# Expert blocks in a straight line, further blocks listed on the chip

## The chip, the cores and the metric
The kernel runs on one core of a Trainium2 chip. TensorE (PE) multiplies, VectorE (DVE), ScalarE (ACT) and GpSimd (POOL) work on elements, SyncE (SP) issues most transfers. The metric is the device time of one execution in microseconds; the median of three runs of the kernel before is 744.07 us (741.57 to 744.4).

## The reference
Causal attention (2 batches, 12 heads, 448 positions, 64 wide), then a dense layer pair with a sigmoid gate, then a routed layer with eight experts, one for each token. The last part is what the change touches:

```
logits = x @ w_gate;  e_idx = argmax(logits, axis=1)        # 896 tokens, 8 experts
gate_w = softmax(logits)[e_idx];  eom = sigmoid(x @ w_output_gate)
for e in range(8):
    mask = e_idx == e
    h = maximum(x[mask] @ w1[e], 0)      # 768 -> 1024
    out[mask] = gate_w[mask] * eom[mask, e] * (h @ w2[e])   # 1024 -> 768
```

With the inputs of the runs the experts get 189, 5, 2, 48, 222, 30, 58 and 342 tokens.

## The kernel before
Attention and the dense layers run to about 404 us and stay as they are. Their output `y1_d` lies in DRAM; beside it DRAM holds a list `xl_d` with 896 places for each expert, into which `place` scatters token number and weight of each 128 tokens as they are routed.

An expert's work comes in **blocks** of up to 128 tokens (`block`, L805). A block gathers its token rows by a list (`gather`, into `xw` or `xr`), transposes them and splits them into a high and a low float32r part (`prep`, into `xh`, `xl`). The weights of an expert are twelve units `u` of 512 KB: six of `w1`, six of `w2` (four of 512 columns, two of 256). A unit is loaded by SP into one of 24 places, so two experts are on the chip (`load32`), and split into a high and a low part in one of six pairs of buffers, `ent` and `entb` (`split`, L275): a cast to float32r, for five units on POOL (L279) and for seven on ACT (L281), and a subtraction on DVE (L282). `l1` multiplies xh by high, xh by low and xl by high (L834, L838); `relu` goes to `hs`, `tr` transposes it and splits it into `hh` and `hl` (L851), and `l2m` does the second product (L858, L860). The output is scaled and scattered to `out` by POOL (L892).

The first block takes the first tokens of expert 0 among the first 640 tokens, before routing is complete (`lw0`), and the other tokens of expert 0 come after it (`le0`). For each expert `rest(o, i)` is an If: where an expert has more than 128 tokens left, a further block runs inside it, with another nested If behind it for the next 128. The count of further blocks of all experts is packed into one number, read into a register of every engine (`load_counts`), and each branch has a prefetch hint some units ahead (`hint`). Then the expert's last block runs, which reloads each place with the weights of the expert after next. Further blocks thus run while their expert's weights are on the chip, and load nothing.

Each engine runs its instructions in the order written, and waits for others by semaphores; POOL's casts, gathers and scatters share one line, and so do DVE's subtractions for weights, for `hl` and for the small operations of routing. Splits run three units ahead of a block, two more at its start.

Of the kernel before, what the change touches and what calls it, by code (L numbers as in the profile page):

```python
# [107 lines left out]
def kernel(ctx, tc, q, k, v, w_in, w_out, w_gate, w_og, w1, w2, out):  # L108
    nc = tc.nc
# [23 lines left out]
    SPLIT_AT = (0, 6, 13)  # L133
    BIG = 65536
    CUT = 5
    POOL_HI, AHEAD, OVER = (3, 5, 7, 9, 11), 5, 3
# [22 lines left out]
    with tc.manual_schedule():  # L159
# [92 lines left out]
        def src_of(e, u):  # L252
            if u < 6:
                hf, kk = u // 3, u % 3 * 2
                return w1[e, kk * 128:(kk + 2) * 128, hf * 512:(hf + 1) * 512].rearrange("(a p) n -> p a n", p=128), 2
            g4, r = (u - 6) // 3 * 4, (u - 6) % 3
            if r < 2:
                kk = g4 + 2 * r
                return w2[e, kk * 128:(kk + 2) * 128, 0:512].rearrange("(a p) n -> p a n", p=128), 2
            return w2[e, g4 * 128:(g4 + 4) * 128, 512:768].rearrange("(a p) n -> p a n", p=128), 4  # L260
# [3 lines left out]

        def load32(o, u):
# [9 lines left out]
        def split(o, u):  # L275
            raw = places[(NU * o + u) % NR]
            hi, lo = entries[u % NENT]
# [213 lines left out]
        for fq in range(4):  # L491
            for fc in range(4):
# [13 lines left out]
                if f == 15:  # L506
                    es_x.close()
                    mp = ctx.enter_context(pool("moe2"))
                    xw_t = [mp.tile([128, DM], F32, name="xw0")]
                    lw_t = [mp.tile([128, NE, 2], I32, name=f"lwin{i}") for i in range(2)]  # L510
                    lr_t = [mp.tile([128, 2], I32, name=f"lr{i}") for i in range(2)]
                    lgB = mp.tile([64, TT, 128], F32, name="lgB")
                    es_gg, ggp = opened(pool("gsplit"))
# [159 lines left out]
        def xpair(n):  # L673
            pl = wp if n else mp
            return [pl.tile([128, KD, 128], F32R, name=f"x{c}{n}") for c in "hl"]

        def prep(xw, pair):
            xh, xl = pair
            for hf in range(2):
                p = ps.tile([128, 4, 128], F32, name="ps_x", tag="tp", bufs=2)  # L680
                for c in range(3):
                    kk = 3 * hf + c
                    nc.tensor.transpose(p[:, c], xw[:, kk * 128:(kk + 1) * 128], ident)
                dst = xh[:, 3 * hf:3 * hf + 3]
                nc.scalar.copy(dst, p[:, 0:3])
                nc.vector.tensor_sub(xl[:, 3 * hf:3 * hf + 3], p[:, 0:3], dst.bitcast(F32))
# [3 lines left out]
        xm = xpair(0)  # L690
# [6 lines left out]
        ix = [mp.tile([128, 1], I32, name=f"ix{i}") for i in range(2)]  # L697

        def cut_count():
# [5 lines left out]
            nc.vector.tensor_scalar(pos0, pos0, c0_f, float(NT * e0), op0=ALU.add, op1=ALU.add)  # L705

        def rest_list(i, lw):
            x = ix[i % 2]
            nc.vector.tensor_scalar(x, pos0, float(128 * i), None, op0=ALU.add)
            nc.vector.memset(lw, BIG)  # L710
            nc.gpsimd.indirect_dma_start(
                out=lw, out_offset=None, in_=xl_d[:, :],
                in_offset=bass.IndirectOffsetOnAxis(ap=x.bitcast(U32), axis=0),
                bounds_check=NT * (e0 + 1) - 1, oob_is_err=False)
# [10 lines left out]
        for t in range(TT):  # L725
# [25 lines left out]
            def h15(t=t):  # L751
                if t == TT - 1:
                    prep(xw_t[0], xm)

            hooks = dict(zip(R_AT, (h2, h5, h7, h10, h15)))
            if t == TT - 1:
                for u, kk in enumerate(SPLIT_AT):
                    hooks[kk] = lambda u=u: split(0, u)
# [5 lines left out]
        xr = wp.tile([128, DM], F32, name="xr")  # L764
        nc.gpsimd.memset(xr, 0.0)
        xx = xpair(1)
# [10 lines left out]
        def rest_lists():  # L777
            rest_list(0, le0)
            rest_list(1, lr_t[1])
            for i in range(2):  # L780
                nc.gpsimd.dma_start(lw_t[i], xl_d.rearrange(
                    "(e r) c -> r e c", e=NE)[128 * i:128 * (i + 1)])


        ci = mp.tile([128, 1], I32, name="ci")

        def counts():
            p = ps.tile([128, 2 * NE], F32, name="ps_tot", tag="sm", bufs=2)
            nc.tensor.matmul(p[:, 0:NE], ones, acc[TT], start=True, stop=True)
            cf = mp.tile([128, NE], F32, name="cf")  # L790
            cw = mp.tile([128, NE], F32, name="cw")
            xf = mp.tile([128, 1], F32, name="xf")
            nb = mp.tile([128, NE], I32, name="nb")
            nc.vector.tensor_add(cf, p[:, 0:NE], cbase)
            nc.vector.tensor_sub(cf[:, e0:e0 + 1], cf[:, e0:e0 + 1], c0_f)
            nc.vector.tensor_copy(nb, cf)
            nc.vector.tensor_scalar(nb, nb, 7, None, op0=ALU.logical_shift_right)
            nc.vector.tensor_copy(cw, nb)
            nc.vector.tensor_mul(cw, cw, pw8)
            nc.vector.tensor_reduce(xf, cw, axis=AX.X, op=ALU.add)  # L800
            nc.vector.tensor_copy(ci, xf)
# [3 lines left out]
        def block(o, pair, lw, final, hooks):  # L805

            xh, xl = pair
            hs = hs_t[npass[0] % 2]
# [7 lines left out]
            def step(u):  # L816
                v = u + AHEAD
                if v < NU:
                    split(o, v)
                    if final and o + 2 < NE:  # L820
                        load32(o + 2, v)
                elif v - NU >= OVER:
                    return
                elif not final:
                    split(o, v - NU)
                elif o + 1 < NE:
                    split(o + 1, v - NU)

            def l1(u):
                hf, k0 = u // 3, u % 3 * 2  # L830
                hi, lo = entries[u % NENT]
                for n in range(2):
                    for m, wt in enumerate((hi, lo)):
                        nc.tensor.matmul(hps[hf], xh[:, k0 + n], wt[:, n], start=k0 + n == 0 and m == 0, stop=False)  # L834
                    if n == 0:
                        hook((hf, k0))
                for n in range(2):
                    nc.tensor.matmul(hps[hf], xl[:, k0 + n], hi[:, n], start=False, stop=k0 + n == KD - 1)  # L838
# [14 lines left out]
            def l2m(py, u, n, kks):  # L853
                hi, lo = (t.rearrange("p a n -> p (a n)").rearrange("p (b n) -> p b n", n=n)
                          for t in entries[u % NENT])
# [6 lines left out]
            for v in range(AHEAD):  # L862
                if v >= OVER:
                    split(o, v)
                if final and o + 2 < NE:
                    load32(o + 2, v)
# [30 lines left out]

        def windows(o):
            return (nblk >> (3 * ORDER[o])) & 7

        def hint(o, i):
            tc.mark_branch_hint_location(f"more{o}_{i}", hint=(windows(o) + (7 - i)) >> 3, engines=engs)

        def rest(o, i):
            with tc.If(windows(o) > i, label=f"more{o}_{i}"):  # L905
                e = ORDER[o]
                lw = lr_t[i % 2] if o == 0 or i > 1 else lw_t[1][:, e]
                prep(xr, xx)
                hooks = {}
                if i + 1 < TT:  # L910
                    lnx = lr_t[(i + 1) % 2]

                    def h0():
                        if o == 0:
                            rest_list(i + 1, lnx)
                        else:
                            window(e, i + 1, lnx)

                    hooks[0, 3] = h0
                    hooks[1, 3] = lambda: gather(lnx, xr)  # L920
                    hooks[6] = lambda: hint(o, i + 1)
                block(o, xx, lw, False, hooks)
                if i + 1 < TT:
                    rest(o, i + 1)

        def load_counts():
            nonlocal nblk
            nblk = nc.values_load(ci[0:1, 0:1], min_val=0, max_val=8 ** NE - 1)

        nblk = None  # L930

        def first_x():
            gather(le0, xw)
            gather(lr_t[1], xr)

        def first_end():
            hint(0, 1)
            prep(xw, xm)

        block(0, xm, lw0, False, {  # L940
            (0, 1): lambda: tr_y(TT - 1, "A"), (0, 2): last_logits, (0, 3): lambda: pick(TT - 1),
            (1, 0): last_place, (1, 4): counts, "b": rest_lists, 7: first_x, 9: load_counts, 10: first_end})
        for o, e in enumerate(ORDER):
            rest(o, 1)
            hooks = {}
            if o + 1 < NE:
                en = ORDER[o + 1]

                def nx(en=en):
                    gather(lw_t[0][:, en], xw)  # L950
                    gather(lw_t[1][:, en], xr)

                hooks[0, 2] = nx
                hooks[9] = lambda: prep(xw, xm)
                hooks[6] = lambda o=o: hint(o + 1, 1)
# [31 lines left out]
```

## Time and profile before
| | |
|---|---|
| median of the runs | 744.07 us |
| profiled execution, its own time | 740.07 us |
| its span, first to last instruction | 738.1 us |
| mean granted clock of TensorE | 0.945 |
| busy over the span: PE, DVE, ACT, POOL | 86%, 67%, 43%, 38% |

The span is what a trace shows; some 2 us of the execution lie around it. Busy shares are means over stages with different limits: attention and the dense layers fill PE nearly, the blocks of experts do not. The page cuts the span in 40 slices; from the 24th on, where the experts are, PE is at six to eight tenths.

### The profile page before, as it was taken

How to read it: one execution, taken by the hardware profiler on the slowest of the kernel's cores; microseconds unless marked ns; L12 is line 12 of the kernel's file. 1: busy time of each engine (PE TensorE's matmuls, PEld its weight loads, DVE VectorE, ACT ScalarE, POOL GpSimd, SP SyncE). 2: the span in 40 equal slices, each digit the busy share in tenths (PEclk: the TensorE clock that was granted, in tenths of full speed). 3: DMA queues.
4: the chain of work that ended last, by engine and by line, in shares of the span. 5: the costliest groups of instructions: out<-in, count | busy, mean ns of one | idle time of the engine just before them, and what ended most of it. 6: DMA issues, size and time to landing. Idle time of an engine off the chain costs nothing. (4 is left out here: it accounts for less than half of the span.)

```text
span 738.1 us, 10610 instructions
## 1 busy us (share of the span) xinstructions
PE 638.1 (86%) x3488; PEld 483.4 (65%) x3488; DVE 492.0 (67%) x872; ACT 318.1 (43%) x662; POOL 283.3 (38%) x331
## 2 busy tenths in 40 slices
PE   8999999999997987799999848688888588788875
PEld 3444444788886877777777636466676466676664
DVE  3667767477778787765446838378678358578854
ACT  5777776233332443433223423344354243444431
POOL 3344343163334275720103255235532424522531
PEclk9999999999999999999999978899999798999999
DMA  7544531153445341365404118479760578200000
GB/s 169 188 94 105 125 85 32 56 151 117 143 140 148 110 133 39 100 216 192 143 15 133 60 52 290 140 257 288 235 218 3 176 261 288 67 11 14 23 17 21
DMA packets 78608, 93.29 MB, mean 126 GB/s; under 512 B 39950, under 2 KB 49070, under 8 KB 78512
## 3 DMA queue, kind: packets, MB, share of 16 engines
q1 hardware_dynamic: 73456, 83.88, 36.9%
q0 software_dynamic: 3040, 5.55, 2.4%
q10 hardware_dynamic: 2016, 2.75, 1.0%
q8 instruction: 40, 0.66, 0.4%
q14 instruction: 56, 0.46, 0.2%
HBM read 91.69 MB, written 7.54 MB: 134 GB/s over the span
## 5 line engine op out<-in xcount | busy, mean ns | idle before, releaser
L557 PE MATMUL py<-slotA,gs 128*128 128x256 f32 (+1 forms) x609 | 115.3, 343 | 1.4 <-POOL gs L488 1.4
L557 PEld LDWEIGHTS py<-slotA,gs 128*128 128x128 f32 x609 | 92.5, 195 | 15.1 <-issue 2.6
L418 PE MATMUL ph<-xhi,slotA 128*128 128x512 f32 (+1 forms) x384 | 96.9, 372 | 4.8 <-DVE g L518 4.8
L228 POOL TENSOR_TENSOR slotA<-w,slotA 128x512 fp32r<-128x512 f32 x45 | 62.0, 1379 | 81.7 <-ACT slotA L226 81.6
L418 PEld LDWEIGHTS ph<-xhi,slotA 128*128 128x128 f32 x384 | 70.2, 189 | 15.1 <-issue 5.8
L834 PE MATMUL ps_h<-ent,xh 128*128 128x512 f32 x192 | 60.8, 435 | 18.3 <-POOL ent L279 13.2
L282 DVE TENSOR_TENSOR ent<-wrb,ent 128x1024 fp32r<-128x1024 f32 x30 | 43.1, 1469 | 43.3 <-POOL ent L279 42.0
L226 ACT CAST slotA<-w 128x512 fp32r<-128x512 f32 x45 | 27.9, 620 | 89.2 <-DVE w L224 89.2
L282 DVE TENSOR_TENSOR ent<-wraw,ent 128x1024 fp32r<-128x1024 f32 x48 | 64.3, 1368 | 1.5 <-POOL ent L279 1.5
L371 POOL TENSOR_SCALAR P<-P,rc 128x64 f32<-128x64 f32 (+2 forms) x72 | 36.8, 513 | 63.7 <-DVE rc L370 53.3
L834 PEld LDWEIGHTS ps_h<-ent,xh 128*128 128x128 f32 x192 | 38.0, 207 | 29.3 <-POOL ent L279 14.5
L347 PE MATMUL sc<-kz,qT 128*64 128x64 f32 (+6 forms) x336 | 55.2, 405 | 0.9 <-ACT kz L337 0.9
L418 PE MATMUL ph<-xlo,slotA 128*128 128x512 f32 x192 | 55.7, 371 | 0.0
L360 DVE TENSOR_REDUCE nmax<-sc 128x1 f32<-128x64 f32 (+6 forms) x84 | 35.5, 423 | 27.6 <-PE sc L349 27.1
L488 DVE TENSOR_TENSOR gs<-g,gs 128x512 fp32r<-128x512 f32 x38 | 31.5, 837 | 32.8 <-ACT gs L486 32.7
L224 DVE SCALAR_TENSOR_TENSOR w<-raw,w 128x512 uint32<-128x512 uint32 x46 | 51.9, 1129 | 1.2
L362 ACT ACTIVATE P<-sc,nmax 128x64 f32<-128x64 f32 (+6 forms) x84 | 40.1, 477 | 27.0 <-DVE nmax L360 14.9
L282 DVE TENSOR_TENSOR ent<-wr,ent 128x1024 fp32r<-128x1024 f32 x18 | 27.1, 1532 | 35.5 <-POOL ent L279 34.3
L892 POOL DMA_INDIRECT out_dram<-hs,lwin x9 | 9.8, 1086 | 103.2 <-ACT hs L891 78.8
L834 PE MATMUL ps_h<-entb,xh 128*128 128x512 f32 x96 | 30.6, 443 | 18.2 <-ACTq L905 16.9
L518 DVE TENSOR_TENSOR g<-ph,g 128x256 f32<-128x256 f32 x64 | 23.6, 389 | 29.2 <-ACT g L517 29.2
L860 PE MATMUL ps_yA<-entb,hl 128*128 128x512 f32 x48 | 19.8, 500 | 26.5 <-DVE hl L851 26.5
(182 smaller groups left out, 1322.7 us busy)
## 6 DMA issues: line engine op xcount, KB each, us to landing
wraw<-in_moe_w_dram SPq DMA_DIRECT2D x44, 512.0 KB, 5.5
wrb<-in_moe_w_dram SPq DMA_DIRECT2D x32, 512.0 KB, 6.1
raw<-in_moe_w_in_dram SPq DMA_DIRECT2D x24, 512.0 KB, 4.1
raw<-in_moe_w_out_dram SPq DMA_DIRECT2D x22, 512.0 KB, 3.5
wr<-in_moe_w_dram SPq DMA_DIRECT2D x20, 512.0 KB, 4.9
qraw<-in_q_dram SPq DMA_DIRECT2D x24, 112.0 KB, 2.9
kraw<-in_k_dram SPq DMA_DIRECT2D x24, 112.0 KB, 2.9
vraw<-in_v_dram SPq DMA_DIRECT2D x24, 96.0 KB, 2.5
```

The lines of the kernel that those rows point to most:

```text
L224: nc.vector.scalar_tensor_tensor(wu, r[:, :, 0], 29, wu, op0=ALU.logical_shift_right, op1=ALU.bitwise_or)
L226: nc.scalar.copy(slot[:, 0], w)
L228: nc.gpsimd.tensor_sub(slot[:, 1], w, slot[:, 0].bitcast(F32))
L282: nc.vector.tensor_sub(lo, raw, hi.bitcast(F32))
L347: nc.tensor.matmul(sc[64 * h:64 * h + 64, :n], qT[:, j * QB:(j + 1) * QB], kT[:, h, :n], start=True, stop=False)
L360: nc.vector.tensor_reduce(nm, sc[:, :n], axis=AX.X, op=ALU.max, negate=True)
L362: nc.scalar.activation(Pb[j][:, :n], sc[:, :n], AF.Exp, bias=nm, scale=1.0, accum_out=sm)
L371: eng[NORM_ENG[j]].tensor_scalar(Pb[j][:, :n], Pb[j][:, :n], rc, 1.0, op0=ALU.mult, op1=ALU.mult)
L418: nc.tensor.matmul(p[:, 0:128 * nt], wt, xt[:, kk, 128 * t0:128 * (t0 + nt)], start=kk == 0 and n == 0, stop=kk == KD - 1 and n == 2)
L488: eng.tensor_sub(gs[:, 1], src, gs[:, 0].bitcast(F32))
L557: nc.tensor.matmul(py[:, :n], gt[:, kk % 4], wt, start=kk == 0 and m == 0, stop=kk == KF - 1 and m == 2)
L834: nc.tensor.matmul(hps[hf], xh[:, k0 + n], wt[:, n], start=k0 + n == 0 and m == 0, stop=False)
```

## The change
All first blocks run one after the other without an If between them: the first block, then one for each expert. Every further block of any expert becomes an entry of a list that the chip makes: `further` (some 48 small DVE operations, issued in pass 2) works out from the counts, for each of up to six entries, which expert it belongs to and where its tokens stand in `xl_d`; POOL fetches the six token lists (`further_lists`). The further blocks run last, in six nested Ifs without hints (`chain`). With the inputs of the runs three of them run. Their weights are loaded again, by an address that SP takes from a register (`bass.ds(e, 1)` in `src_of`). Loads are written for the pass after next in every pass, also inside the Ifs, whether or not that later block runs.

All casts go to ACT. Two of the twelve units, 0 and 3 (`WHOLE`), are not split: PE multiplies the raw f32 weights with an f32 copy `xf` of the first two chunks of x. Splits are numbered through all passes and rotate over the six buffer pairs; five run ahead at all times.

```diff
-    POOL_HI, AHEAD, OVER = (3, 5, 7, 9, 11), 5, 3
+    WHOLE, AHEAD, NOV = (0, 3), 5, 6
         def load32(o, u):
-            src, parts = src_of(ORDER[o], u)
+            src, parts = src_of(ORDER[o] if o < NE else over[o - NE], u)
+        def again(o, u, last):
+            if last and o + 2 < NE + NOV:
+                load32(o + 2, u)
+        passes = [(0, False)] + [(o, True) for o in range(NE + NOV)]
+        order = [(p, u) for p in range(len(passes)) for u in range(NU) if u not in WHOLE]
+        def split():
+            if nsplit[0] == len(order):
+                return
+            p, u = order[nsplit[0]]
+            hi, lo = entry_of[p, u] = entries[nsplit[0] % NENT]
+            nsplit[0] += 1
+            o, last = passes[p]
             raw = places[(NU * o + u) % NR]
-            if u in POOL_HI:
-                nc.gpsimd.tensor_scalar(hi, raw, 1.0, 1.0, op0=ALU.mult, op1=ALU.mult)
-            else:
-                nc.scalar.copy(hi, raw)
+            nc.scalar.copy(hi, raw)
             nc.vector.tensor_sub(lo, raw, hi.bitcast(F32))
+            again(o, u, last)
...
+        def further():
+            nc.vector.tensor_copy(nb, cnt)
+            nc.vector.tensor_scalar(nb, nb, 7, None, op0=ALU.logical_shift_right)
...
+            for e in range(NE):
+                nc.vector.tensor_add(pt[:, e + 1:e + 2], pt[:, e:e + 1], x[:, e:e + 1])
...
+            for b in range(NOV):
+                nc.vector.tensor_scalar(sel[:, b], pt, float(b), None, op0=ALU.is_le)
+            nc.vector.tensor_sub(oh, sel[:, :, 0:NE], sel[:, :, 1:1 + NE])
...
+            nc.vector.tensor_copy(ix[:, 0:NOV], r)
...
+            nc.vector.tensor_copy(ci, f)
+        def further_lists():
+            for b in range(NOV):
+                list_at(b, lo_t[b], NT * NE)
             def step(u):
-                v = u + AHEAD
...
+                if u in WHOLE:
+                    again(o, u, last)
+                else:
+                    split()
             def l1(u):
+                if u in WHOLE:
+                    raw = places[(NU * o + u) % NR]
+                    for n in range(2):
+                        nc.tensor.matmul(hps[hf], xf[:, n], raw[:, n], start=n == 0, stop=False)
+                        hook((hf, n))
+                    return
...
-        for o, e in enumerate(ORDER):
-            rest(o, 1)
...
+        def some(p):
+            if p + 1 < len(passes):
+                hooks[0, 2] = lambda: gather(lists[p + 1], xw)
+                hooks[10] = lambda: prep(xw)
+            if p == 2:
+                hooks[1, 1] = further
+                hooks[9] = further_lists
+            if p == 5:
+                hooks[0, 0] = lambda: over.extend(
+                    nc.values_load(ci[0:1, b:b + 1], engines=[ET.SP], min_val=0, max_val=NE - 1)
+                    for b in range(NOV))
+            if p == NE:
...
+                hooks[8] = load_nov
+            block(lists[p], hooks)
+        def chain(b):
+            with tc.If(nov > b):
+                some(1 + NE + b)
+                if b + 1 < NOV:
+                    chain(b + 1)
+        for p in range(1, NE + 1):
+            some(p)
+        chain(0)
```

The first place is POOL's line in one block. Before, from the start of the last block of expert 0 to its scatter (`ent`, `entb` are split buffers, `wr`, `wraw`, `wrb` places of raw weights):

```order
L279 TENSOR_SCALAR ent_4401<-wr_3745 128x1024
L279 TENSOR_SCALAR ent_4427<-wraw 128x1024
L668 DMA xw_3076<-y_d,lwin_3077 128x768
L668 DMA xr<-y_d,lwin_3078 128x768
L279 TENSOR_SCALAR entb<-wraw 128x1024
L279 TENSOR_SCALAR ent_4401<-wraw 128x1024
L279 TENSOR_SCALAR ent_4427<-wrb_3913 128x1024
L902 REGISTER_ALU x2
L902 ISA
L982 BRANCH_PREFETCH_HINT
L892 DMA out_dram<-hs_4521,le_3110 896x768
```

POOL after, from the first pass's list of remaining tokens through the scatter of pass 1:

```order
L727 DMA le_3108<-xl_d,ix 128x2
L792 DMA lwin<-xl_d 128x8x2
L686 DMA xw_3076<-y_d,le_3108 128x768
L933 DMA out_dram<-hs_4523,lw_3107 896x768
L686 DMA xw_3076<-y_d,lwin 128x768
L933 DMA out_dram<-hs_4524,le_3108 896x768
L686 DMA xw_3076<-y_d,lwin 128x768
L726 MEMSET lo_3113 128x2
L727 DMA lo_3113<-xl_d,ix 128x2
L726 MEMSET lo_3114 128x2
```

The casts and the gather for a possible further block have left POOL's line, and between two scatters one gather stands, with the memsets and fetches of six lists once.

The second place is DVE's line at `hl`, before, in one further block of the nested Ifs (L282 subtracts for a split):

```order
L282 TENSOR_TENSOR entb<-wraw,entb 128x1024
L282 TENSOR_TENSOR ent_4387<-wraw,ent_4386 128x1024
L851 TENSOR_TENSOR hl<-ps_hT,hh 128x512
L282 TENSOR_TENSOR ent_4402<-wraw,ent_4401 128x1024
L282 TENSOR_TENSOR ent_4418<-wraw,ent_4417 128x1024
L282 TENSOR_TENSOR ent_4428<-wraw,ent_4427 128x1024
L902 REGISTER_ALU x2
L902 ISA
L982 BRANCH_PREFETCH_HINT
L851 TENSOR_TENSOR hl<-ps_hT,hh 128x512
L282 TENSOR_TENSOR entb<-wrb_3913,entb 128x1024 x2
```

DVE after, in pass 2 from the middle of `further` to the `hl` behind it (L300 subtracts for a split, `oht`, `ohr`, `ohf` are small tiles of `further`, `ix` the list addresses, `ci` the numbers read into registers):

```order
L832 TENSOR_TENSOR oht<-oh,val 128x8 x6
L833 TENSOR_REDUCE ohr<-oht 128x6
L834 CAST ohf<-pidx_i 128x1
L836 TENSOR_SCALAR ohr<-ohr,ohf 128x1 x6
L838 CAST ix<-ohr 128x6
L840 TENSOR_TENSOR oht<-oh,eidx 128x8 x6
L841 TENSOR_REDUCE ohf<-oht 128x6
L842 COPY ohf<-pt 128x1
L843 CAST ci<-ohf 128x7
L897 TENSOR_TENSOR hl<-ps_hT,hh 128x512
L300 TENSOR_TENSOR ent_4406<-wraw,ent_4405 128x1024
```

Before, six subtractions stand between a block's `xl` and the first `hl`; after, three do, and in this one pass the operations of `further` as well.

## Rows read from the trace of the kernel before

**Rows 1.** Stretches: bounds, length, busy PE, PEld, DVE, ACT, POOL, clock, DMA, GB/s
```profile
436.00:738.00 302.00, 232.57 (x1085) 187.01 (x1083) 202.23 (x173) 122.07 (x164) 115.16 (x87) 0.90 0.44 144
500.00:530.00 30.00, 23.32 (x112) 18.83 (x111) 22.07 (x19) 12.41 (x17) 14.88 (x12) 0.94 0.82 263
```

**Rows 2.** Groups, 436 to 738 us: count, busy us, mean ns, idle before
```profile
L842 ACT ACTIVATE hs<-ps_h 128x512 f32<-128x512 f32 x22 | 13.2, 599 | 55.2 <-PE ps_h L838 41.3 <-DMA out_dram<-hs,lwin 8.3 <-DMA out_dram<-hs,lw 5.7
```

**Rows 3.** Waits, 436 to 738 us: total us, times, longest
```profile
PE ps_yA L860 <- DVE hl L851: 26.5, 11, 3.4
PE ps_h L834 <- ACTq L905: 16.9, 8, 3.1
PE ps_h L834 <- POOL ent L279: 13.2, 3, 6.3
```

**Rows 4.** Timeline of PE, 548 to 572 us: start, length, instructions, wait before
```profile
548.73 1.20 PE L834 MATMUL ps_h<-entb,xh 128*128 128x512 f32 x4 [0.34 <-ACT xh L685]
...
557.66 1.35 PE L858 MATMUL ps_yA<-entb,hh 128*128 128x512 f32 x4
...
561.76 1.22 PE L860 MATMUL ps_yA<-entb,hl 128*128 128x512 f32 x2 [2.75 <-DVE hl L851]
...
566.89 1.09 PE L858 MATMUL ps_yA<-ent,hh 128*128 128x512 f32 x4
...
568.28 1.10 PE L858 MATMUL ps_yA<-ent,hh 128*128 128x512 f32 x4
...
571.92 0.50 PE L834 MATMUL ps_h<-entb,xh 128*128 128x512 f32 x1 [0.67 <-ACTq L905]
```

**Rows 5.** Groups on PE, whole span, the plain f32 products of attention
```profile
L347 PE MATMUL sc<-kz,qT 128*64 128x448 f32 x48 | 11.7, 564 | 0.0
...
L347 PE MATMUL sc<-kz,qT 128*64 128x128 f32 x48 | 5.3, 298 | 0.0
```

**Rows 6.** Groups, 436 to 738 us, the subtractions and casts of splits
```profile
L282 DVE TENSOR_TENSOR entb<-wraw,entb 128x1024 fp32r<-128x1024 f32 x16 | 26.1, 1637 | 6.6 <-POOL entb L279 6.6
...
L281 ACT CAST ent<-wraw 128x1024 fp32r<-128x1024 f32 x22 | 22.8, 1038 | 0.0
...
L282 DVE TENSOR_TENSOR entb<-wr,entb 128x1024 fp32r<-128x1024 f32 x8 | 9.6, 1215 | 0.8 <-ACT entb L281 0.7
```

**Rows 7.** DMA, 440 to 630 us: packets, MB, share; KB each, us to landing
```profile
q1 hardware_dynamic: 22656, 37.75, 60.3%
q0 software_dynamic: 1618, 2.48, 4.0%
...
wrb<-in_moe_w_dram SPq DMA_DIRECT2D x24, 512.0 KB, 6.0
```

**Rows 8.** Timeline of the first pass, 398 to 443 us
```profile
408.26 0.68 DVE L599 COPY yT<-ps_yT 128x512 f32<-128x512 f32 x1
...
424.51 1.10 POOL L711 DMA_INDIRECT le<-xl_d,ix  x1 [4.24 <-DVE lr L710]
...
428.82 1.11 POOL L279 TENSOR_SCALAR ent<-wrb 128x1024 fp32r<-128x1024 f32 x1
...
430.12 2.07 POOL L668 DMA_INDIRECT xw<-y_d,le  x1 [0.18 <-issue]
...
431.85 1.22 PE L860 MATMUL ps_yA<-ent,hl 128*128 128x512 f32 x2 [7.29 <-DVE hl L851]
...
435.21 0.82 PE L683 MATMUL ps_x<-ident,xw 128*128 128x128 f32 x6
...
440.47 1.20 PE L834 MATMUL ps_h<-entb,xh 128*128 128x512 f32 x4 [3.08 <-ACTq L905]
```

**Rows 9.** Timeline of DVE there, first and last of eight small operations
```profile
421.45 0.16 DVE L794 TENSOR_TENSOR cf<-ps_tot,cbase 128x8 f32<-128x8 f32 x1
...
422.86 0.15 DVE L801 CAST ci<-xf 128x1 int32<-128x1 f32 x1
```

**Rows 10.** Timeline of PE at the end of the span
```profile
730.70 0.62 PE L860 MATMUL ps_yB<-ent,hl 128*128 128x256 f32 x4
```

More of the change, by code (lines that the diff above doesn't have):

```diff
@@ L696 @@
         pos0 = mp.tile([128, 1], F32, name="pos0")
-        ix = [mp.tile([128, 1], I32, name=f"ix{i}") for i in range(2)]
+        ix = mp.tile([128, 1 + NOV], I32, name="ix")
+        lo_t = [mp.tile([128, 2], I32, name=f"lo{i}") for i in range(NOV)]
         def cut_count():
@@ L803, with block @@
+            nc.vector.tensor_copy(ix[:, 0:NOV], r)
+            for b in range(NOV):
+                nc.vector.tensor_mul(t[:, b], oh[:, b], eidx)
+            nc.vector.tensor_reduce(f[:, 0:NOV], t, axis=AX.X, op=ALU.add)
+            nc.vector.tensor_copy(f[:, NOV:NOV + 1], pt[:, NE:NE + 1])
+            nc.vector.tensor_copy(ci, f)
+        def further_lists():
+            for b in range(NOV):
+                list_at(b, lo_t[b], NT * NE)
         npass = [0]
-        def block(o, pair, lw, final, hooks):
-            xh, xl = pair
-            hs = hs_t[npass[0] % 2]
+        def block(lw, hooks):
+            o, last = passes[npass[0]]
+            p0 = npass[0]
+            hs = hs_t[p0 % 2]
@@ L816, in step @@
             def step(u):
-                v = u + AHEAD
[L818 to L827, printed above, removed]
+                if u in WHOLE:
+                    again(o, u, last)
+                else:
+                    split()
             def l1(u):
                 hf, k0 = u // 3, u % 3 * 2
-                hi, lo = entries[u % NENT]
+                if u in WHOLE:
[4 more added lines that the diff above has]
+                    return
+                hi, lo = entry_of[p0, u]
                 for n in range(2):
                     for m, wt in enumerate((hi, lo)):
-                        nc.tensor.matmul(hps[hf], xh[:, k0 + n], wt[:, n], start=k0 + n == 0 and m == 0, stop=False)
+                        nc.tensor.matmul(hps[hf], xh[:, k0 + n - 2], wt[:, n], start=False, stop=False)
                     if n == 0:
@@ L854, in l2m @@
                 hi, lo = (t.rearrange("p a n -> p (a n)").rearrange("p (b n) -> p b n", n=n)
-                          for t in entries[u % NENT])
+                          for t in entry_of[p0, u])
                 for b, kk in enumerate(kks):
@@ L896 @@
         engs = (ET.PE, ET.DVE, ET.Pool, ET.Activation, ET.SP)
[L898 to L930, printed above, removed]
+        lists = [lw0, le0] + [lwin[:, e] for e in ORDER[1:]] + lo_t
         def first_x():
             gather(le0, xw)
[L934 to L940, printed above, removed]
+        block(lw0, {
             (0, 1): lambda: tr_y(TT - 1, "A"), (0, 2): last_logits, (0, 3): lambda: pick(TT - 1),
-            (1, 0): last_place, (1, 4): counts, "b": rest_lists, 7: first_x, 9: load_counts, 10: first_end})
```

139 lines of the change are left out of this document (69 added, 70 removed).

## The prediction

> **What bounds the kernel now.** The order of reading was: engine shares over the stretch of the expert blocks, the waits inside it, then one block instruction by instruction, and last the first pass and the tail. The stretch from 436 us to the end is 302 us long; PE is busy for 232.6 us of it at a mean granted clock of 0.90, and the DMA engines for 0.44 of it [rows 1]. 22 Relus of half a block each stand in it, so it holds 11 blocks [rows 2]: eight last blocks of experts and three further ones, 27.5 us each. No engine is full, so the waits decide. PE's largest are 26.5 us for `hl` from DVE, 16.9 us behind the branch of an If (eight of them) and 13.2 us for POOL's casts [rows 3].
>
> What a block would cost without waits is read from the one at 548.73 to 571.92 (23.2 us), an If body [rows 4]. Its six W1 units and four transposes take 8.93 us. Two neighbouring W2 units start 1.39 us apart, the price of six float32r products. The last unit, of 256 columns, then takes 1.58 us to where PE waits 0.67 us for the branch. The rest is one wait of 2.75 us for `hl` and what follows it: the next two products take 1.22 us, where a third of 1.39 is 0.46. From 557.66 to 571.92 there are 14.26 us; less the waits 10.84; four units at 1.39, two at 1.58 and four transposes at about 0.6 make 9.3, so 1.5 us is lost to the slower matmuls behind the wait.
>
> **Part by part.** *Two raws of twelve as f32.* Units 0 and 3 of a block become two f32 products each, in place of six float32r products. The nearest f32 products come as two records per product and grow from 298 ns at 128 columns to 564 at 448, 0.83 ns a column [rows 5]; four records of 512 columns are 1.70 us, 1.75 with gaps. Against 1.39 this adds 0.35 a unit. Bounds: 0.93 us if a record went at the pace of a float32r product (1.39/6), 2.47 if records did not overlap at all (617 ns each), so -0.5 to +1.1 a unit, -10 to +24 us over the 22 units of eleven blocks; I take +8, since the slope is of the same type of operands. Ten splits stay instead of twelve.
>
> *The pass.* A block then has four W1 units at 1.39, two f32 units at 1.75, four W2 units at 1.39, two at 1.58, and 14 transposes at 0.14 (six of them took 0.82 [rows 8]): 5.56 + 3.50 + 5.56 + 3.16 + 1.96 = 19.7 us. I take 20.0.
>
> *All casts on ACT, none on POOL.* Ten casts at 1.04 are 10.4 us, and two Relus at 0.60 [rows 2], two `hh`, two outputs, `xf` and `xh`, all of about that size, add 4.5: 15 of 20 us. DVE's subtraction takes 1.22 us in one group and 1.64 mean in another that shares its time with POOL's casts [rows 6]. At 1.22 ten are 12.2 us, with `hl` and `xl` 14.3. Both fit below PE. Five splits now run ahead across the block's border, and `hl` stands directly behind a split whose cast ACT did long before, so the `hl` wait (26.5), POOL's cast waits (13.2) go; nothing that PE needs is behind POOL except the gather, which has some 15 us before its transposes. What is late next is `xf`, which ACT copies behind an output and a cast about when the next pass starts; up to 0.5 us, inside the 20.0.
>
> *The Ifs.* Six skipped bodies disappear; PE stood 16.9 us at eight [rows 3], 3.08 at the first [rows 8]. The body that was entered cost 0.34 [rows 4]. Three entries remain, now without a hint, between 0.34 and 3.1 each: I take 1 each, 3 us, near the entered one. That the last, skipped branch has to fetch code hides under the last scatter. The Trainium skill (Runtime: NRT & Kernel Launch, Instruction fetch mechanics) says that a branch to code outside the fetched pages stalls for a fetch. By it the sum would take up to 3.1 us more a branch, 9 in all, where the entered body of this trace shows almost none.
>
> *First pass.* Today pass 1 starts at 440.47 [rows 8]. PE stood 7.29 us for `hl` at 431.85, because DVE waited for POOL's cast of 428.82, which was behind POOL's list transfers; then 3.08 for the branch. Both go. The gather of `xw`, issued at 430.12 and used 5.1 us later, then decides: it can go out right behind the list issue of 424.51 + 1.10 at the earliest, as now at the latest; I take 427.5, so transposes at 432.6. The copy of `yT` (408.26), on which all lists hang, stood behind a backlog of splits; with most done earlier I take 2 us off. With the copy of `xf` pass 1 starts at 432, between 428 and 436.
>
> *Lists on the chip.* 48 small DVE operations enter pass 2, between a split and `hl`. Eight such took 1.56 us, 0.195 each [rows 9]; independent ones are shorter, so 5 to 9.4 us, I take 8. DVE reaches them when units 0 to 2 (4.5 us), a Relu, a cast and a subtraction are through, 7.4 us into the pass; 8 more and 0.7 for `hl` make 16.1. PE wants it after six W1 units, four transposes and four products: 3.5 + 5.56 + 0.56 + 0.93 = 10.5. That is 5.6 us of wait once, and 1.5 of slow matmuls behind it as in the block above. POOL's six lists have six passes to land.
>
> *Loads.* Of 24 places each is loaded anew when split. Five further experts' weights are loaded (65 loads by register, the last 29 for blocks that never run), 137 loads in all from pass 0 on, 71.8 MB. In 440 to 630 us the queue moved 37.75 MB in 60.3% of 190 us, 329 GB/s while busy: 19.1 us for an expert's 6.29 MB; gathers and scatters took 4.0%, below 1 us a block [rows 7]. So 20 us a block of DMA against 20 of PE: even, and with two experts in hand the needed loads are never late. But the end waits for the unneeded ones: eight loads can be under way, 12.7 us, of which the tail covers 6.8. I add 3 us, between 0 and 8. The Trainium skill (DMA: Bandwidth & Descriptors, Where 436 GB/s comes from) gives about 358 GB/s per core from HBM: 17.6 us an expert (an estimate), with which the loads would leave 2 us of slack in every pass and the 3 us would vanish. The trace differs, and counts.
>
> **Sum.** 432 + 11 x 20.0 + 5.6 + 1.5 + 3 = 662 for PE's last matmul. Today the end is 6.8 us behind it (731.3 to 738.1 [rows 10]); with 3 for the loads the span is 672, with the 2 us outside it 674. That is against the profiled execution's 740.07; the median of the runs shown is 744.07, 0.54% more, so 678.
>
> **Rivals.** *Loads decide.* The first reload follows a split in the second half of pass 0, about 424 us. If DMA holds only 263 GB/s with everything in the way, 71.8 MB take 273 us, the last landing at 697; with 3 us of end and 2 outside, and 0.54%, 706. For it: PE and DMA are even, and the stretch from 500 to 530 us moved that much at a share of 0.82 [rows 1]. Against it: there the queue was not always fed, and it does 329 when it is [rows 7].
>
> *The passes stay at 23.2 us.* ACT with all casts, or DVE, falls behind as POOL's share comes to them, or the entries come free late: 432 + 255 + 10 + 6.8 + 2 = 706, 710 with 0.54%. For it: ACT has 15 instructions more in line before `xf`. Against it: both keep 5 us idle.
>
> *Slower.* The place is SP from about 545 us on (432 + 5.65 x 20, the second half of pass 6), when loads address weights by a register. If such a load waited for its own landing before the next (6.0 us median [rows 7]), 65 take 390 us: the end near 940. From 2.9 us a load on (545 + 65 x 2.9 = 734) it ends later than today. Against it: it is the same queue and shape, only the start address differs; for it: the trace has no load of this kind.
>
> **Chances.** Forecast 0.76, loads 0.11, passes at 23.2 0.06, slower 0.05, others near no change 0.02. The forecast's own range, from the f32 bounds taken half (-5 to +12), the start (-4 to +4) and the branches (+6), is 664 to 694. The range for 8 in 10 reaches into the two middle rivals: 662 to 706. About 0.5% is what a measurement can tell from no change: faster 0.93, within it 0.02, slower 0.05.
>
> **What would show it.** Relu pairs every 20 us from 432 on with one gap at pass 2; no wait of PE for `hl` but there; f32 records of about 0.43 us spacing; subtractions all near 1.22; a granted clock near 1 from 440 on; DMA above 0.9 busy to the end and nothing on PE waiting for it; POOL with gathers and scatters alone. Wrong would be: casts of ACT that wait for a load, a spacing of Relu pairs above 22 us, or loads from 545 on that issue slower than those before.

## The result and the profile after

| | before | after |
|---|---|---|
| median of the runs, us | 743.12 (4 runs, 741.57 to 744.4) | 665.62 (4 runs, 664.68 to 667.08) |
| profiled execution, its span, us | 740.07, 738.1 | 667.08, 665.1 |
| granted clock, mean over the span | 0.945 | 0.976 |
| busy PE, DVE, ACT, POOL | 86, 67, 43, 38% | 94, 67, 53, 30% |

After by before is 0.896, interval 0.893 to 0.899: 77 us less. The forecast was 678 us with a range from 662 to 706; it came out 12 us too slow. The stretches of after, with the columns of [rows 1] (bounds, length, busy PE, PEld, DVE, ACT, POOL, clock, DMA share, GB/s):

```profile
430.00:665.00 235.00, 216.58 (x1040) 166.68 (x1040) 157.86 (x193) 150.38 (x201) 38.80 (x35) 0.95 0.93 325
500.00:530.00 30.00, 30.00 (x139) 22.34 (x138) 20.99 (x20) 20.33 (x29) 5.09 (x4) 1.00 0.93 324
```

In 500 to 530 us PE is busy for all 30.00 us, against 23.32 in [rows 1]; DVE and ACT keep a third free, and the DMA engines are at 0.93. Now one engine is full, and the blocks cost what its products cost. The waits of PE over 430 to 665 us (total, times, longest):

```profile
PE ps_x L694 <- DMA xw<-y_d,le: 5.1, 1, 5.1
PE ps_yA L906 <- DVE hl L897: 4.0, 1, 4.0
```

That is the answer to [rows 3]: one wait for the gather ahead of pass 1, one for `hl` in pass 2, none for an If and none for POOL. One ordinary pass is read from PE's timeline (start, length, instructions):

```profile
524.36 1.88 PE L874 MATMUL ps_h<-wr,xf 128*128 128x512 f32 x4
526.08 0.60 PE L894 MATMUL ps_hT<-ident,hs 128*128 128x128 f32 x4
526.43 1.18 PE L880 MATMUL ps_h<-ent,xh 128*128 128x512 f32 x4
...
530.25 0.64 PE L906 MATMUL ps_yA<-entb,hl 128*128 128x512 f32 x2
...
532.55 1.11 PE L904 MATMUL ps_yB<-ent,hh 128*128 128x256 f32 x8
...
533.98 1.10 PE L904 MATMUL ps_yA<-ent,hh 128*128 128x512 f32 x4
...
535.38 1.10 PE L904 MATMUL ps_yA<-ent,hh 128*128 128x512 f32 x4
...
536.78 0.38 PE L694 MATMUL ps_x<-ident,xw 128*128 128x128 f32 x2
...
537.36 1.18 PE L904 MATMUL ps_yB<-ent,hh 128*128 128x256 f32 x8
...
538.94 1.98 PE L874 MATMUL ps_h<-wrb,xf 128*128 128x512 f32 x4
...
543.55 1.88 PE L874 MATMUL ps_h<-wrb,xf 128*128 128x512 f32 x4
```

From f32 unit 3 (524.36) to the same place one pass on (543.55) there are 19.19 us, and no row carries a wait. Differences of starts give the units: f32 1.72, a unit of 256 columns 1.43 (the last one of a pass 1.58, 537.36 to 538.94), one of 512 columns 1.40, four transposes 0.35, six transposes of x 0.58. The first Relus of passes stand 19.17 us apart throughout, but for 25.9 between passes 2 and 3. There DVE works through `further`, and PE stands:

```profile
463.00 0.17 DVE L817 CAST nb<-cnt 128x8 int32<-128x8 f32 x1
...
469.42 0.68 DVE L897 TENSOR_TENSOR hl<-ps_hT,hh 128x512 fp32r<-128x512 f32 x1
```

```profile
470.15 1.22 PE L906 MATMUL ps_yA<-entb,hl 128*128 128x512 f32 x2 [4.01 <-DVE hl L897]
...
471.88 2.05 PE L904 MATMUL ps_yA<-entb,hh 128*128 128x512 f32 x4
...
476.43 1.10 PE L904 MATMUL ps_yA<-ent,hh 128*128 128x512 f32 x4
```

```profile
470.15:476.40 6.25, 6.25 (x24) 5.37 (x25) 5.58 (x6) 2.58 (x3) 5.26 (x8) 0.57 0.60 180
```

The lists take 6.4 us of DVE, and PE waits 4.01. The same work that takes 3.73 us in the ordinary pass (530.25 to 533.98) then takes 6.28 (470.15 to 476.43), at a granted clock of 0.57 over that stretch. The largest group of subtractions, 430 to 665 us, to compare with [rows 6]:

```profile
L300 DVE TENSOR_TENSOR ent<-wraw,ent 128x1024 fp32r<-128x1024 f32 x41 | 49.8, 1223 | 39.4 <-ACT ent L299 39.0
```

Every group of subtractions has a mean of 1.22 us, where one group of before stood at 1.64 [rows 6]. Loads by register (550 us to the end), and below them those of the same kernel that still have a fixed address (450 to 545 us):

```profile
q1 hardware_dynamic: 22015, 36.62, 91.1%
...
wraw<-in_moe_w_dram SPq DMA_DIRECT2D x30, 512.0 KB, 6.4
```

```profile
wraw<-in_moe_w_dram SPq DMA_DIRECT2D x23, 512.0 KB, 7.3
```

For the places `wr`, `wraw` and `wrb` landing takes 6.4, 6.4 and 6.8 us by register, and 5.8, 7.3 and 6.9 us by a fixed address. 67 loads go out in these 115 us, one every 1.7 us, while one takes over 6 to land: nothing is serialised. The end:

```profile
653.48 0.63 PE L906 MATMUL ps_yB<-ent,hl 128*128 128x256 f32 x4
...
656.07 1.53 POOL L933 DMA_INDIRECT out_dram<-hs,lo  x1 [16.34 <-ACTq L968]
```

PE is done at 654.1, the span ends at 665.1.

### The profile page after: what moved, and what is told of

Read it like the earlier page. It is cut to its first block, busy times and chain, and to the rows that moved or that the text cites. A ratio compares the mean times of both kernels' runs of the same rounds, so it can differ in the third digit from the quotient of the medians.

```text
span 665.1 us, 10285 instructions
## 1 busy us (share of the span) xinstructions
PE 624.6 (94%) x3446; PEld 463.4 (70%) x3446; DVE 444.8 (67%) x881; ACT 351.0 (53%) x705; POOL 196.8 (30%) x271
## 3 DMA queue, kind: packets, MB, share of 16 engines
q10 hardware_dynamic: 2016, 2.75, 1.2%
## 4 chain that ended last, share of the span: by engine, by line
PE 41%; issue 23%; DVE 17%; DMA 9%; ACT 6%; POOL 2%; ACTq 0%; POOLq 0%; DVEq 0%
PE py L575 11%; PE sc L366 8%; DMA out_dram<-hs,lwin 6%; DVE w L224 5%; DVE w L221 4%; PE ps_o L416 4%; PE ps_pT L398 4%; PE ph L437 4%; DVE w L219 3%; DVE g L536 2%; DMA out_dram<-hs,lo 2%; ACT g L535 2%; PE sc L368 2%; PE ps_tr L348 2%; PE ps_h L874 1%
## 5 line engine op out<-in xcount | busy, mean ns | idle before, releaser
L300 DVE TENSOR_TENSOR ent<-wraw,ent 128x1024 fp32r<-128x1024 f32 x45 | 54.7, 1223 | 40.7 <-ACT ent L299 40.4
L366 PE MATMUL sc<-kz,qT 128*64 128x64 f32 (+6 forms) x336 | 57.3, 418 | 0.8 <-ACT kz L356 0.7
L224 DVE SCALAR_TENSOR_TENSOR w<-raw,w 128x512 uint32<-128x512 uint32 x46 | 51.9, 1129 | 1.2
L299 ACT CAST ent<-wraw 128x1024 fp32r<-128x1024 f32 x45 | 46.7, 1047 | 0.0
L505 ACT CAST gs<-g 128x512 fp32r<-128x512 f32 x56 | 33.1, 617 | 15.2 <-PE py L575 9.4
L880 PE MATMUL ps_h<-ent,xh 128*128 128x512 f32 x128 | 39.3, 428 | 0.0
L221 DVE SCALAR_TENSOR_TENSOR w<-raw,w 128x512 uint32<-128x512 uint32 x46 | 38.1, 828 | 1.6
L437 PEld LDWEIGHTS ph<-xlo,slotA 128*128 128x128 f32 x192 | 35.5, 191 | 4.6
L300 DVE TENSOR_TENSOR entb<-wraw,entb 128x1024 fp32r<-128x1024 f32 x22 | 26.8, 1224 | 17.1 <-ACT entb L299 16.9
```

What stands on the lines that cost most here:

```text
L221: nc.vector.scalar_tensor_tensor(wu, r[:, :, 1], 0xC0000000, wu, op0=ALU.bitwise_and, op1=ALU.bitwise_or)
L224: nc.vector.scalar_tensor_tensor(wu, r[:, :, 0], 29, wu, op0=ALU.logical_shift_right, op1=ALU.bitwise_or)
L366: nc.tensor.matmul(sc[64 * h:64 * h + 64, :n], qT[:, j * QB:(j + 1) * QB], kT[:, h, :n], start=True, stop=False)
L437: nc.tensor.matmul(p[:, 0:128 * nt], wt, xt[:, kk, 128 * t0:128 * (t0 + nt)], start=kk == 0 and n == 0, stop=kk == KD - 1 and n == 2)
L880: nc.tensor.matmul(hps[hf], xh[:, k0 + n - 2], wt[:, n], start=False, stop=False)
```

## Experiments
All kernels are the changed one with an edit, or the one before with an edit where it says so. Each ratio is to the kernel before on the same chip (medians there 742.5 to 744.4).

**Casts back on POOL.**
```diff
+            if u in (5, 7, 9, 11):
+                nc.gpsimd.tensor_scalar(hi, raw, 1.0, 1.0, op0=ALU.mult, op1=ALU.mult)
+            else:
                 nc.scalar.copy(hi, raw)
```


> The changed kernel, but the casts of units 5, 7, 9 and 11 go back to POOL. Theory (the waits for hl came from the short lead of splits and from the Ifs, POOL's casts only carried them): with five splits ahead the blocks stay PE-bound at 19.2 us, DVE's subtractions beside POOL's casts grow to 1.6 to 2.0 us but fit, and the time is 665 to 671 us. Rival (POOL's casts in themselves made hl late, 26.5 + 13.2 us of PE's waits over eleven blocks): a wait for hl of 2 to 3 us comes back in each block, 22 to 40 us with the slower matmuls behind it, 688 to 705 us.

663.87 us, ratio 0.894 (0.891 to 0.897). The groups of subtractions rise to means of 1.33 to 1.47 us, passes take 19.01, and outside pass 2 no wait for `hl` comes back. In this form of the kernel POOL's casts cost nothing.

**The same, three splits ahead across a block's border.**
```diff
+            if p0:
+                split()
+                split()
             for u in range(6):
...
-                else:
+                elif u < 10:
                     split()
```


> The changed kernel with POOL casting units 5, 7, 9 and 11 and with the splits' lead cut as it was before: the last two units of a block split nothing, and two splits stand at the block's start. Theory (the lead of five across the border is what removed the wait for hl): with three ahead hl stands behind five or six subtractions beside POOL's casts, a wait of 2 to 3 us returns in each block, 690 to 705 us. Rival (in a straight line POOL is never late, so the lead does not matter): passes stay at 19.0 to 19.3 us, 663 to 669 us.

663.39 us, 0.894 (0.890 to 0.898), passes of 19.03 to 19.10; PE waits for `hl` in pass 2 alone (7.0 us). So in this form the lead isn't needed either.

**The kernel before with all casts on ACT**, and nothing else.
```diff
-            if u in POOL_HI:
+            if u in ():
```


> The kernel before with all twelve casts on ACT, nothing else changed (nested Ifs, two splits at a block's start). Theory (before, POOL's casts made DVE late, since there they stand behind scatters and gathers with little lead): the six subtractions before hl take 1.22 us each, hl is ready when PE wants it, the waits for hl (26.5 us) and for POOL's casts (13.2) shrink to a few us and the time is 690 to 705 us. Rival (the Ifs and their merges made the waits, as the straight line with POOL's casts at 663.9 us suggests): less than 12 us is gained, 730 us or more.

685.56 us, 0.924 (0.920 to 0.928): 57 of the 77 us come from this line alone, more than expected. Its waits of PE, 430 to 690 us:

```profile
PE ps_h L834 <- ACTq L905: 19.5, 8, 3.4
PE ps_x L683 <- DMA xw<-y_d,le: 6.1, 1, 6.1
```

No wait for `hl` is left, while the Ifs' waits are as large as in [rows 3]. So POOL's casts cost 57 us in one kernel and nothing in the other; the next three runs look for what differs.

**All twelve raws split** (no f32 products).
```diff
-    WHOLE, AHEAD, NOV = (0, 3), 5, 6
+    WHOLE, AHEAD, NOV = (), 5, 6
```
(`prep` makes `xh` and `xl` in two halves of three chunks, and the small tiles of `further` lie in another pool.)

> The changed kernel with no f32 raws: all twelve units are split, xh and xl hold all six chunks of x, nothing else moves. Theory (PE sets the pass, the f32 units cost 0.33 us each): 24 units give 7 to 8 us back, a pass of 18.5 us, 656 to 660 us; the loads then need 340 GB/s. Rival (ACT and DVE set the pass once they have twelve splits: 12 casts at 1.05 and 12 subtractions at 1.22 with their other work are 17 us each, and the gaps between instructions come on top): the pass is 19.5 us or longer, casts come late for PE, 668 to 685 us.

665.74 us, 0.897 (0.895 to 0.900). Passes take 18.96 us where 18.5 were expected: of the 0.64 that two f32 units cost, only 0.2 comes back, since at each pass's start PE's second group of products stands ready later (1.35 us after the first, 555.60 to 556.95, where 0.94 is the rule) behind `xl`. Without an earlier `xl` the f32 products neither gain nor lose time.

**Twelve splits, POOL's five casts, three ahead**, so all that the kernel before does to its weights, in a straight line; **and the same with five ahead**.
```diff
+            if u in (3, 5, 7, 9, 11):
+                nc.gpsimd.tensor_scalar(hi, raw, 1.0, 1.0, op0=ALU.mult, op1=ALU.mult)
```
(on the kernel with all twelve split; the first one with the lead's edit from above too)

> The changed kernel with all twelve raws split, POOL's casts back for five of the units (3, 5, 7, 9, 11) and only three splits ahead across the border of two blocks, as the kernel before has it: so all that the kernel before does to its weights, but in a straight line without Ifs. Theory (the Ifs made POOL's casts late: POOL meets them behind gathers, scatters and merges of the nested bodies): the passes stay within 18.9 to 19.5 us, no wait for hl over 0.5 us outside pass 2, 663 to 672 us. Rival (twelve subtractions with POOL's casts among them are simply too much for DVE before hl): a wait for hl of 2 to 3.4 us returns in every pass, passes of 21.5 to 23 us, 690 to 710 us.

> As the one beside it, but with five splits ahead as in the changed kernel. Theory (Ifs): the same time within 3 us, 663 to 670 us, passes 18.9 to 19.3 us. Rival (too much for DVE before hl): the two further splits ahead take two subtractions, 2.5 to 3.3 us, out of DVE's way to hl, so that the wait is gone here and this kernel is 20 us or more faster than the one with three ahead.

718.64 us, 0.965 (0.961 to 0.969), with three ahead, more than either side expected; 675.55 us, 0.908 (0.904 to 0.912), with five. The theory that the Ifs made POOL's casts late falls: without Ifs the wait is back, and passes take 24.3 us. Two splits more ahead are worth 43 us, though some 0.74 us of wait a pass stays (passes of 20.0). The run with three ahead also tells what the straight line with its list is worth by itself: 26 us (744.37 us before on that chip), where the casts alone gave 57. Why the wait is back, POOL's, DVE's and PE's timelines of that run show:

```profile
563.92 1.06 POOL L937 DMA_INDIRECT out_dram<-hs,lwin  x1 [15.27 <-ACT hs L936]
565.02 2.06 POOL L300 TENSOR_SCALAR ent<-wrb 128x1024 fp32r<-128x1024 f32 x2
```

```profile
566.11 5.19 DVE L303 TENSOR_TENSOR ent<-wrb,ent 128x1024 fp32r<-128x1024 f32 x3 [2.97 <-POOL ent L300]
571.22 2.06 DVE L303 TENSOR_TENSOR entb<-wrb,entb 128x1024 fp32r<-128x1024 f32 x1
573.21 2.06 DVE L303 TENSOR_TENSOR entb<-wraw,entb 128x1024 fp32r<-128x1024 f32 x1
575.19 1.21 DVE L303 TENSOR_TENSOR ent<-wraw,ent 128x1024 fp32r<-128x1024 f32 x1
576.33 0.68 DVE L898 TENSOR_TENSOR hl<-ps_hT,hh 128x512 fp32r<-128x512 f32 x1
```

```profile
577.06 0.73 PE L907 MATMUL ps_yA<-entb,hl 128*128 128x512 f32 x2 [2.76 <-DVE hl L898]
```

POOL's first cast of a block is written behind the scatter of the block before, and the scatter waits for that block's last output. So DVE idles 2.97 us for the cast, and only then starts on six subtractions, four of which take some 2.06 us while POOL casts; `hl` is seventh. By these rows PE's wait (2.76) is shorter than the idle time (2.97) and than the slowing (4 x 0.85 = 3.4): without either one it would be gone (an estimate; no run has one without the other). The Trainium skill (SBUF — State Buffer, Who interferes with whom) says that a VectorE instruction with two inputs in SBUF contends with a GpSimd one that reads SBUF, since they share a port pair under an exclusive lock. 2.06 against 1.21 us agrees with it. The kernel before has the same order, in the block of [rows 4] (its PE waits 2.75), with DVE idle for 1.07 us and again six subtractions before `hl`, four of them of some 2.06 us; there the slowing weighs more:

```profile
548.58 1.09 POOL L892 DMA_INDIRECT out_dram<-hs,lwin  x1 [12.81 <-ACT hs L891]
549.72 1.05 POOL L279 TENSOR_SCALAR ent<-wr 128x1024 fp32r<-128x1024 f32 x1
```

```profile
550.80 4.04 DVE L282 TENSOR_TENSOR ent<-wr,ent 128x1024 fp32r<-128x1024 f32 x2 [1.07 <-POOL ent L279]
...
561.03 0.68 DVE L851 TENSOR_TENSOR hl<-ps_hT,hh 128x512 fp32r<-128x512 f32 x1
```

With two raws as f32, three ahead and POOL's casts, the scatter delays the first cast in the same way, but fewer subtractions follow:

```profile
559.29 1.23 DVE L303 TENSOR_TENSOR entb<-wraw,entb 128x1024 fp32r<-128x1024 f32 x1 [2.92 <-POOL entb L300]
560.44 1.22 DVE L303 TENSOR_TENSOR ent<-wraw,ent 128x1024 fp32r<-128x1024 f32 x1
562.61 3.19 DVE L303 TENSOR_TENSOR ent<-wraw,ent 128x1024 fp32r<-128x1024 f32 x2 [0.96 <-POOL ent L300]
565.73 0.68 DVE L900 TENSOR_TENSOR hl<-ps_hT,hh 128x512 fp32r<-128x512 f32 x1
```

Four stand before `hl` in place of six, and it comes just in time (ready at 566.41, used at 566.49). So the wait of before needs three things together: twelve splits, casts on POOL, and a lead of three. The change removes all three. Each was taken away once: the short lead in the run with five ahead, POOL's casts in the kernel before with ACT's, and two splits in the run just shown, where POOL also has four casts in place of five, so that fewer splits and fewer casts are not told apart. Without any one of them the wait is gone, but for 0.74 us a pass where only the lead is longer.

**Skipped Ifs in the straight line.**
```diff
+            if p >= 4:
+                with tc.If(nv > NOV - 1):
+                    nc.vector.memset(zz[:, 0:1], 0.0)
+                    nc.gpsimd.memset(zz[:, 1:2], 0.0)
+                    nc.scalar.copy(zz[:, 2:3], cut_f)
```
(five small bodies, between passes, never entered; PE has a branch at each, but no instruction in a body)

> The changed kernel with the number of further blocks read once more after pass 3 and five Ifs after passes 4 to 8, whose body (one tiny operation each on DVE, POOL and ACT) is never entered. Theory (a skipped body costs PE what it did before, 16.9 us at eight, 2.1 each, because the engine has to jump and fetch): 8 to 13 us more, 674 to 679 us. Rival (it was the distance of the jump over six nested bodies and the waits set for their transfers; a short jump is nearly free): 0.5 us each or less, 665 to 669 us.

667.33 us, 0.899 (0.895 to 0.903), passes still of 19.17 us. A short skipped body costs nothing that shows, so what the eight branches of before cost (16.9 us, [rows 3]) is not a branch by itself. The trace of the kernel before tells more, here from one of the eight (PE's and ACT's timelines, then line L905, the If, with start times):

```profile
497.95 1.19 PE L834 MATMUL ps_h<-entb,xh 128*128 128x512 f32 x4 [2.84 <-ACTq L905]
498.10 1.05 ACT L281 CAST ent<-wr 128x1024 fp32r<-128x1024 f32 x1 [2.42 <-ACTq L905]
```

```profile
L905 PEldq EVENT_SEMAPHORE  x1: 51/51/51, 495.2 to 495.2; - x1
L905 ACTq COMPARE_BRANCH  x1: 49/49/49, 495.3 to 495.3; - x1
L905 ACTq EVENT_SEMAPHORE  x1: 17/17/17, 497.9 to 497.9; - x1
```

PE is past its own branch at 495.2. ACT takes its branch at 495.3 and gives its signal behind the If at 497.9; all but its last output (done at 495.7) is idle time. PE waits for that signal. Five of the eight waits are of this kind (2.81 to 3.08 us, with 2.5 to 2.8 between ACT's branch and signal); in the other three (0.67 to 0.74 us) ACT needs 0.4 to 0.5. By these rows PE pays, where the engines meet, for ACT's way over the skipped body. With the small bodies ACT goes on working between branch and signal. The Trainium skill (Runtime: NRT & Kernel Launch, Instruction fetch mechanics) has a taken branch stall where its target lies outside the pages already fetched; skips of three instructions that cost nothing agree with it, and no run here shows that ACT's 2.5 us are such a fetch.

**The lists' DVE work in two halves**, in passes 2 and 3, each behind `hl`.
```diff
+        def further_b():
...
             if p == 2:
-                hooks[1, 1] = further
-                hooks[9] = further_lists
+                hooks[7] = further
+            if p == 3:
+                hooks[7] = further_b
+            if p == 4:
+                hooks[9] = further_lists
```


> The changed kernel with the 48 small DVE operations of the block list in two halves, each behind the second hl of a pass (passes 2 and 3), POOL's lists a pass or two later. Theory (the 6.7 us by which pass 2 is longer is the wait for hl and the slow matmuls behind it): both go, 5 to 7 us less, 659 to 661 us. Rival (DVE has too little room in a pass, its work is late anyway): the wait moves to a subtraction of the next pass, less than 2 us gained.

661.44 us, 0.891 (0.889 to 0.894): 4.2 us less than after. The two passes take 20.35 and 19.62 us, and 1.1 us of waits of PE, for `xl`, are left of this.

**Three further blocks in place of six**, so nothing is loaded for blocks that never run.
```diff
-    WHOLE, AHEAD, NOV = (0, 3), 5, 6
+    WHOLE, AHEAD, NOV = (0, 3), 5, 3
```


> The changed kernel with room for three further blocks instead of six, which is what these inputs need, so that the last two passes load nothing for blocks that never run, and the last splits for such a block go too. Theory (the end waits for the last loads, 3.6 us beyond the old tail of 6.8): PE's last matmul stays, the tail shrinks from 10.4 to about 7 us, 661 to 663 us. Rival (the tail is the last scatter and leaving six nested Ifs, not the loads): the tail stays above 9.5 us and the time within 1.5 us of 665.6.

658.04 us, 0.887 (0.884 to 0.889). The stretch from 625 to 658 us, columns as above, and the last product:

```profile
625.00:658.00 33.00, 25.12 (x132) 19.94 (x130) 15.35 (x15) 14.80 (x21) 2.52 (x2) 0.92 0.05 21
```

```profile
649.49 0.63 PE L906 MATMUL ps_yB<-ent,hl 128*128 128x256 f32 x4
```

DMA is idle (0.05), and the span ends 6.2 us behind PE (650.1 to 656.3), not 11.0. The 4.8 us between have two parts, by the last output of the changed kernel and the last scatter of this run:

```profile
655.30 0.49 ACT L932 ACTIVATE hs<-ps_yB,lo 128x256 f32<-128x256 f32 x1
```

```profile
650.97 0.99 POOL L933 DMA_INDIRECT out_dram<-hs,lo  x1 [15.88 <-ACT hs L932]
```

In the changed kernel the last scatter starts 2.0 us behind PE's end (654.1 to 656.07), here 0.9: there ACT, before it makes the last output, copies x and casts weights for a block that never runs, 1.1 us. And the scatter lands 6.5 us after its issue there, beside the loads, against 2.9 here, 3.6 us. So unneeded loads cost 3.6 us at the end, and other unneeded work 1.1. This run has no skipped If at its end either; in the changed kernel that branch holds PE to 657.9, before the scatter's landing (662.6), so it doesn't show. Of the rest, 2.0 us are shorter lists in pass 2 (23.9 us in place of 25.9).

**The best of these**: all twelve split, lists in halves, and `prep` one unit earlier.
```diff
-                hooks[10] = lambda: prep(xw)
+                hooks[9] = lambda: prep(xw)
...
+            if p == 4:
+                hooks[8] = further_lists
```


> The changed kernel with all twelve units split, the list operations in two halves in passes 2 and 3, and the transposes of the next x one unit earlier, so that xl is ready when PE starts a pass (with all units split, PE waited 0.6 us for it in each). Theory (PE sets the pass once xl is early): a pass of 18.4 to 18.5 us, 8 us from the passes and 4 from the lists, 652 to 656 us. Rival (ACT and DVE, each busy 17 us, are late somewhere else): passes of 18.9 us or more, 658 to 662 us.

654.85 us (651.95 to 656.57), 0.881 (0.878 to 0.885): 11 us faster than after, with room for six further blocks as there. Passes without the lists take 18.2 to 18.3 us, 0.9 below after: with `xl` in time the price of the f32 units (0.64) does come back, and a little more. Its stretch from 610 to 650 us:

```profile
610.00:650.00 40.00, 31.74 (x176) 26.91 (x174) 30.04 (x31) 28.48 (x38) 6.48 (x4) 0.94 1.04 375
```

DMA is full now, at 375 GB/s. Gathers and scatters have a share of it; the queue of the loads in the same stretch:

```profile
q1 hardware_dynamic: 8145, 13.72, 95.4%
```

13.72 MB in 40 us are 343 GB/s, 360 while the queue is busy, at which an expert's 6.29 MB take 17.5 us (an estimate). So little is left below 18.2.

## Why the prediction was right, and where it missed

The forecast's case came true: straight passes, and no wait of PE but the two that it named, for the gather ahead of pass 1 and for `hl` in pass 2. Against the profiled execution its sum was 674 us, 6.9 above 667.1. Five terms, each as predicted and as measured:

- **The pass, 20.0 us: 19.17.** Eleven times 0.83 is 9.1 us, the largest miss. The f32 units were right (+0.35 predicted, 1.72 - 1.40 = +0.32 measured), and so was the spacing of their records (0.43 us). Too dear were 14 transposes (1.96 predicted; 0.35 + 0.36 + 0.58 = 1.29), priced by the length of a row of six (0.82) where the difference of starts counts (0.58); the units of 256 columns (1.58 predicted; 1.43 and 1.58, mean 1.51), priced up to a point where PE waited; and the 0.3 of margin. W1 and the wide W2 units took 0.3 more than twice 5.56.
- **Lists, 5.6 + 1.5 us: 4.0 + 2.6.** The sum was right within 0.5; DVE took 6.4 us for the operations (8 predicted: eight in a chain took 1.52 us, 0.19 each, but three groups of six independent ones 0.53 to 0.55, 0.09 each), and the matmuls behind the wait lost more.
- **Three Ifs, 3 us: nothing.** No wait for a branch stands in after, and the Relus of the further blocks keep the spacing of 19.17.
- **Start of pass 1, 432 us: 434.84**, and 1.5 us more for slow products behind the 5.1 us wait for the gather, which weren't priced (6.29 us from the first product to the first Relu, 4.81 in an ordinary pass). The order of events was right, and the gather decides: it went out at 426.64 (427.5 predicted), and PE's transposes started at 433.53 (432.6 predicted), so that it took 6.9 us from issue to use where 5.1 was taken over from [rows 8]. The copy of `yT` came not 2 us earlier but 1.5 later (409.79 against 408.26); it waited for PE, not for splits. But this execution lies 2.5 us behind already at the gather of `xw` ahead of it (399.57 against 397.06), at work which the change leaves alone.
- **The end, 9.8 us: 11.0.** The loads cost 3.6 us (3 predicted, 0 to 8 given), as the run with three further blocks shows; the 1.1 us of ACT's unneeded work weren't in the sum.

The rows of the start of pass 1:

```profile
426.64 1.82 POOL L686 DMA_INDIRECT xw<-y_d,le  x1 [1.21 <-PE ps_yA L904]
```

```profile
433.53 0.66 PE L694 MATMUL ps_x<-ident,xw 128*128 128x128 f32 x2 [5.10 <-DMA xw<-y_d,le]
...
434.84 3.45 PE L874 MATMUL ps_h<-wr,xf 128*128 128x512 f32 x4
```

-9.1 - 0.5 - 3 + 2.8 + 1.5 + 1.2 = -7.1, the whole of it; that 12.6 us too dear and 5.5 too cheap cancel in part is luck. The rest of the 12 us is the scaling: 0.54% (3.6 us) was added, since the profiled execution of before was the shorter one, while that of after is 1.5 us longer than its median. The forecast's own range, 664 to 694, has a slip: its bounds (9 us down, 22 up) were laid around the span of some 672 us. Around the 678 of the forecast they give 669 to 700, and the measured 665.62 lies below that; the range of 662 to 706 holds it.

The first pass aside, the failed step is a reason more than a number. The prediction has the `hl` wait go because five splits run ahead *and* ACT casts; it did not see that each does it alone (but for 0.74 us a pass with the lead), nor that the two f32 raws, for which it charged 8 us and no gain, are a third way to the same. They cost what was charged (11 x 2 x 0.32 = 7.0 us) and free two subtractions a pass in exchange, which nothing needs once the casts are on ACT.

The rivals: *loads decide* didn't come, with 322 GB/s and a DMA share of 0.93 over 430 to 610 us, nowhere a wait of PE for weights. The queue can do more than the 329 GB/s taken from [rows 7]: 360 while busy, in the last kernel above. The figure of the Trainium skill that was weighed (DMA: Bandwidth & Descriptors, Where 436 GB/s comes from; about 358 GB/s) was the nearer one, if too low for all queues together (375); but the 3 us at the end, which should have vanished by it, became 3.6. *Passes at 23.2* didn't come; it is what the kernel with twelve splits, POOL's casts and three ahead does (24.3). *Serialised loads* didn't come.

## What to carry to other kernels
When a wait has one name, look for all that has to hold for it: here the number of splits, the engine of the casts and the lead had to meet, to change any one was enough, and a one-line edit of the old kernel was worth 57 of 77 us. An engine that does elementwise work for the next block as well as this block's output transfer can make the next block wait for this one's end, as POOL did here; move one of them, or run further ahead. Price a pass by differences of starts in its undisturbed middle, not by the lengths of rows, which overlap, nor by rows next to a wait.

## What the runs showed of the hardware
- A wait of PE costs more than its length. Behind 2.76 us (577.06 in the run with three ahead) the granted clock is 0.68 over the next 5.3 us (part of them at 1.2 GHz, the rest at 2.4), and the work there takes 5.37 us in place of 3.73; behind 4.01 us it is 0.57 over 6.25 us, and 6.28 in place of 3.73. A pass of 24.3 us against 18.96 is 2.76 + 0.95 of two smaller waits + 1.64 of this.
- The queue of the 512 KB loads moved 329 GB/s while busy where it was busy 60.3% of the time [rows 7], 350 where it was 91.1% (after, 550 us on) and 360 where it was 95.4% (the last kernel, 610 to 650 us): in this case the rate read from the queue with gaps was too low.
- A start address from a register costs a load nothing that shows (6.4 to 6.8 us to landing, against 5.8 to 7.3 by a fixed address in the same kernel).
